# Issuing the K and V loads on ScalarE's queue, with the stores left on SyncE's, in an attention backward kernel

## Chip, cores, metric

One core of a Trainium2 chip. The metric is the device time of one execution in microseconds (us), as the median of several executions. A run counts as slow when it is over 1.5% above the fastest of the same kernel. The experiments ran in several batches; before was run again in each, and its median was 646.2 to 646.4 us every time, so times of different batches can be compared. A ratio is the mean time of one kernel's fast runs over that of the other's in the same rounds, so it is not quite the ratio of the medians that stand beside it.

## The reference

One query row per head attends to 8,192 keys; the kernel returns the output and the gradients of q, k and v.

```python
# B=1, H=32 heads, Sq=1, Skv=8192, Dh=128, all bfloat16
def _fwd_reference(q, k, v):
    scale = q.shape[-1] ** -0.5
    attn = softmax(einsum('bhqd,bhkd->bhqk', q, k) * scale, axis=-1)
    return einsum('bhqk,bhkd->bhqd', attn, v)

def reference(q, k, v, grad_out):
    out, vjp = jax.vjp(_fwd_reference, q, k, v)
    return (out, *vjp(grad_out))          # out, dq, dk, dv
```

K and V (2 MB per head each) are read once, dk and dv (2 MB each) are written once: 268 MB in all, with little arithmetic.

## The kernel before

```python
def load_k(h):                                   # 2 MB; the first head's K in 4 parts
    Kt[h] = kpool.tile([P, NT, D], BF16, ...)    # 3 buffers
    nc.sync.dma_start(slots(Kt[h], c, parts), rows_of(k, h, c, parts))
def load_v(h):
    Vt[h] = vpool.tile([P, NT, D], BF16, ...)    # 2 buffers
    nc.sync.dma_start(Vt[h][:], rows_of(v, h, 0, 1))

# narrow matmuls: 64 + 64 + 64 + 64 of a head's 302
def k_scores(h):     # 64 x (128x128 weights, 4 columns)
    for g in range(CH):
        for c in range(2 * NB):
            nc.tensor.matmul(out[:, g, :], lhsT=cols[:, g, c // 2, c % 2], rhs=q_blk[:, h, c, :], ...)
def v_scores(h, c):  # 4 calls x 16 x (128x128 weights, 2 columns)
    ...
def contract(Xt, rep, out_col, first=0, last=NT):   # for V and for K: 64 x (128x128 weights, 1 column)
    for n in range(first, last):
        nc.tensor.matmul(out_col, lhsT=Xt[:, n, :], rhs=rep[:, n, 0:1], ...)

def outer(h, which, r):            # a quarter of dk or dv on VectorE; the last quarter issues the store
    nc.vector.tensor_tensor(slots(G, r, 4)..., op=ALU.mult)      # G: 2 buffers for dk, 2 for dv
    if r % (4 // parts) == 4 // parts - 1:
        nc.sync.dma_start(rows_of(dst, h, c, parts), slots(G, c, parts))

for h in range(H + 1):             # a software pipeline: head h beside the end of head h-1
    ...                            # K blocks and scores of h; ds, dk and dq of h-1
    if 0 < h and h + 2 < H: load_k(h + 2)
    ...                            # softmax; dk's last quarters and its store
    contract(Vt[h], x["p"], x["m"][:, 2:3])
    ...                            # V transposes and v_scores
    outer(h, "dv", 0); outer(h, "dv", 1); outer(h, "dv", 2)
    if 0 < h and h + 2 < H: load_v(h + 2)
    outer(h, "dv", 3)              # issues dv's store
```

So the one queue carries load V, store dv, load K, store dk, and so on, in turn.

Of the kernel before, what the change touches and what calls it, by code (L numbers as in the profile page):

```python
# [23 lines left out]
def kernel(  # L24
# [11 lines left out]
    nc = tc.nc  # L36
# [23 lines left out]
    Kt, Vt, XK, XV, st = {}, {}, {}, {}, {}  # L60

    def rows_of(x, h, c, parts):
        L = NT // parts
        return x[0, h].rearrange("(p n) d -> p n d", p=P)[:, c * L:(c + 1) * L, :]

    def slots(X, c, parts):
        L = NT // parts
        return X[:, c * L:(c + 1) * L, :]

    def load_k(h):  # L70
        Kt[h] = kpool.tile([P, NT, D], BF16, tag="K", name="Kt")
        parts = NCH if h == 0 else 1
        for c in range(parts):
            nc.sync.dma_start(slots(Kt[h], c, parts), rows_of(k, h, c, parts))

    def load_v(h):
        Vt[h] = vpool.tile([P, NT, D], BF16, tag="V", name="Vt")
        nc.sync.dma_start(Vt[h][:], rows_of(v, h, 0, 1))

    rows = consts.tile([H, 2, D], BF16)  # L80
    nc.sync.dma_start(rows[:, 0, :], q.rearrange("b h s d -> (b h s) d"))
    nc.scalar.dma_start(rows[:, 1, :], grad_out.rearrange("b h s d -> (b h s) d"))
    load_k(0)
    load_v(0)
    load_k(1)
    load_v(1)

    ident = consts.tile([P, P], BF16)
# [166 lines left out]
    for h in range(H + 1):  # L255
# [19 lines left out]
        if 0 < h and h + 2 < H:  # L275
            load_k(h + 2)
# [44 lines left out]
        if 0 < h and h + 2 < H:  # L321
            load_v(h + 2)
# [38 lines left out]
```

## Time and profile before

| | before |
|---|---|
| time, median of 3 (range) | 646.56 us (646.2 to 646.75) |
| profiled span | 644.5 us |
| busiest engine | VectorE, 78% |
| DMA share, 120 to 320 us | 1.01, 428 GB/s |

The prediction below shows the lines that carry this. Two more lines are of use. The first is the chain of work that ended last, by line, in the profile of before: it follows back from the end what each step waited for. The second is from the view of waits (time in total, times, longest).

```profile
DMA Kt<-in_k_dram 48%; DVE XK_sb L146 8%; PE T_ps L183 8%; DMA out_dram<-G_dv 5%; DMA out_dram<-G_dk 5%; PE s_ps L157 5%; DVE G_dk L210 4%; PE dp_ps L200 3%; PE m_ps L200 2%; PE dp_ps L195 2%; ACT XT_sb L185 1%; PE m_ps L294 1%; DVE G_dv L210 1%; PE s_ps L173 1%; DVE sm L163 1%
...
DVE G_dv L210 <- DMA out_dram<-G_dv: 84.6, 25, 4.6
```

The chain runs through a K load and back into the computation that freed its buffer; VectorE also waits for the store of dv two heads ago to free its buffer (84.6 us in 25 waits).

### The profile page before, as it was taken

What the parts mean: (1) busy time and instruction counts of PE and PEld (TensorE: products, weight loads), DVE (VectorE), ACT (ScalarE), POOL (GpSimd) and SP (SyncE); (2) the same over time, 40 slices, a digit from 0 to 9 for tenths busy, and PEclk for the clock granted to TensorE, in tenths of its full rate; (3) what the DMA queues carried; (4) which work ended last, traced back from release to release, by engine and by line L of the source; (5) the groups of instructions that cost most, each with busy time, mean ns of one, the idle gap of its engine ahead of it and who ended that gap; (6) DMA issues with size and microseconds to landing.
All of it is one profiled execution on the core that took longest, in us unless ns stands there. A gap on an engine that the chain in (4) does not pass through costs nothing.

```text
span 644.5 us, 20935 instructions
## 1 busy us (share of the span) xinstructions
PE 481.0 (75%) x9673; PEld 452.0 (70%) x9673; DVE 505.5 (78%) x653; ACT 183.5 (28%) x332; POOL 0.7 (0%) x6
## 2 busy tenths in 40 slices
PE   3898888886677877768777787667786777877780
PEld 2888888886677866768666777667785676866670
DVE  5989899867977779777788777797767977778860
ACT  2333333332233222233222332223322223222230
POOL 0000000000000000000000000000000000000000
PEclk9766666655666655666556666556655666655665
DMA  8999999999999999999999999999999999999985
GB/s 349 407 425 430 424 425 423 429 426 431 427 428 427 427 427 429 429 429 425 433 422 433 425 430 427 427 429 425 427 429 425 431 425 429 429 427 430 424 365 238
DMA packets 19718, 269.80 MB, mean 419 GB/s; under 512 B 2352, under 2 KB 2352, under 8 KB 2864
## 3 DMA queue, kind: packets, MB, share of 16 engines
q1 hardware_dynamic: 19584, 268.47, 98.2%
q8 instruction: 75, 1.23, 0.7%
q14 instruction: 11, 0.09, 0.0%
q10 hardware_dynamic: 48, 0.01, 0.0%
HBM read 134.23 MB, written 134.23 MB: 417 GB/s over the span
## 4 chain that ended last, share of the span: by engine, by line
DMA 59%; PE 21%; DVE 14%; ACT 2%; issue 1%; SPq 0%; DVEq 0%; ACTq 0%
DMA Kt<-in_k_dram 48%; DVE XK_sb L146 8%; PE T_ps L183 8%; DMA out_dram<-G_dv 5%; DMA out_dram<-G_dk 5%; PE s_ps L157 5%; DVE G_dk L210 4%; PE dp_ps L200 3%; PE m_ps L200 2%; PE dp_ps L195 2%; ACT XT_sb L185 1%; PE m_ps L294 1%; DVE G_dv L210 1%; PE s_ps L173 1%; DVE sm L163 1%
## 5 line engine op out<-in xcount | busy, mean ns | idle before, releaser
L210 DVE TENSOR_TENSOR G_dv<-p_rep,qd 128x2048 bf16<-128x2048 bf16 x128 | 148.2, 1221 | 90.3 <-DMA out_dram<-G_dv 84.6
L183 PE MATMUL T_ps<-ident_f,Vt 128*128 128x128 f32 x1024 | 203.4, 382 | 0.2 <-PE m_ps L294 0.2
L183 PEld LDWEIGHTS T_ps<-ident_f,Vt 128*128 128x128 f32 x1024 | 190.7, 210 | 0.2 <-issue 0.2
L185 ACT COPY XT_sb<-T_ps 128x1024 f32<-128x1024 f32 x128 | 128.6, 1013 | 129.3 <-PE T_ps L183 127.2
L210 DVE TENSOR_TENSOR G_dk<-ds_rep,qd 128x2048 bf16<-128x2048 bf16 x128 | 155.6, 1218 | 2.9 <-DMA out_dram<-G_dk 1.9
L146 DVE STREAM_TRANSPOSE XK_sb<-Kt 128x1024 f32<-128x1024 f32 x128 | 148.3, 1214 | 5.8 <-DMA Kt<-in_k_dram 4.7
L157 PEld LDWEIGHTS <-XK_sb 128*128 128x128 bf16 x2048 | 57.7, 104 | 90.7 <-DVE pdt L234 79.9
L157 PE MATMUL s_ps<-q_blk,XK_sb 128*128 128x4 bf16 x2048 | 59.7, 168 | 82.1 <-DVE pdt L234 72.1
L195 PE MATMUL dp_ps<-do_blk,XT_sb 128*128 128x2 bf16 x2048 | 66.7, 164 | 18.1 <-ACT XT_sb L185 18.1
L195 PEld LDWEIGHTS <-XT_sb 128*128 128x128 bf16 x2048 | 64.9, 102 | 20.7 <-ACT XT_sb L185 20.7
L200 PE MATMUL dp_ps<-ds_rep,Kt 128*128 128x1 bf16 x2048 | 64.1, 165 | 1.3 <-issue 1.0
L200 PEld LDWEIGHTS <-Kt 128*128 128x128 bf16 x2048 | 59.6, 104 | 6.8 <-issue 6.6
L244 ACT COPY dq_all<-dp_ps 128x1 f32<-128x1 f32 x32 | 5.1, 159 | 192.4 <-PE dp_ps L200 178.5
L200 PEld LDWEIGHTS <-Vt 128*128 128x128 bf16 x2048 | 57.7, 97 | 0.9
L200 PE MATMUL m_ps<-p_rep,Vt 128*128 128x1 bf16 x2048 | 56.9, 164 | 0.0
L294 PEld LDWEIGHTS m_ps<-rs,ones_f 128*128 128x128 f32 x64 | 16.0, 311 | 49.9 <-ACT e L293 49.9
L294 PE MATMUL m_ps<-rs,ones_f 128*128 128x1 f32 x64 | 18.8, 362 | 40.5 <-ACT e L293 40.5
L303 ACT ACTIVATE p_rep<-e,rinv 128x256 bf16<-128x256 f32 x32 | 16.3, 508 | 30.1 <-DVE rinv L301 30.1
L163 DVE TENSOR_TENSOR sm<-s_ps,in_quad 128x256 f32<-128x256 f32 x32 | 13.6, 424 | 11.1 <-PE s_ps L157 7.9
L229 ACT CAST qd<-s_ps 128x256 bf16<-128x256 f32 x32 | 11.9, 372 | 32.2 <-PE s_ps L225 32.2
L236 DVE SCALAR_TENSOR_TENSOR ds_rep<-dp_ps,pdt,p_s 128x256 bf16<-128x256 f32 x32 | 15.5, 484 | 5.2 <-PE dp_ps L195 2.4
L293 ACT ACTIVATE e<-s_ps,nbias 128x64 f32<-128x64 f32 x32 | 10.0, 313 | 31.8 <-DVE nbias L290 31.8
(44 smaller groups left out, 143.4 us busy)
## 6 DMA issues: line engine op xcount, KB each, us to landing
Vt<-in_v_dram SPq DMA_DIRECT2D x32, 2048.0 KB, 30.0
Kt<-in_k_dram SPq DMA_DIRECT2D x31, 2048.0 KB, 30.8
out_dram<-G_dv SPq DMA_DIRECT2D x30, 2048.0 KB, 34.6
out_dram<-G_dk SPq DMA_DIRECT2D x30, 2048.0 KB, 33.6
out_dram<-G_dv SPq DMA_DIRECT2D x4, 1024.0 KB, 15.0
out_dram<-G_dk SPq DMA_DIRECT2D x4, 1024.0 KB, 13.3
Kt<-in_k_dram SPq DMA_DIRECT2D x4, 512.0 KB, 5.1
out_dram<-fin_sb SPq DMA_DIRECT2D x2, 8.0 KB, 13.1
```

The costliest lines, as they stand in the source:

```text
L146: nc.vector.transpose(XK[h][:, :, :, u, :], slots(Kt[h], u, NCH).rearrange("p g d -> p (g d)").bitcast(F32).rearrange("p (g w j) -> p g w ...
L157: nc.tensor.matmul(out[:, g, :], lhsT=cols[:, g, c // 2, c % 2], rhs=q_blk[:, h, c, :], start=(c == 0), stop=(c == 2 * NB - 1), skip_group ...
L163: nc.vector.tensor_tensor(x["sm"][:], x["s"][:, 0:NT].rearrange("p (a g) -> p a g", a=NQ).unsqueeze(2) .to_broadcast([P, NQ, NCH, CH]), in ...
L183: nc.tensor.transpose(T_ps[:, i, :], words[:, m * P:(m + 1) * P], ident_f[:])
L185: nc.scalar.copy(X[:], T_ps[:])
L195: nc.tensor.matmul(st[h]["dp"][:, n:n + 2], lhsT=X[:, i, e2, :], rhs=do_blk[:, h, e2, :], start=(e2 == 0), stop=(e2 == 1), skip_group_chec ...
L200: nc.tensor.matmul(out_col, lhsT=Xt[:, n, :], rhs=rep[:, n, 0:1], start=(n == 0), stop=(n == NT - 1), skip_group_check=True)
L210: nc.vector.tensor_tensor(slots(G, r, 4).rearrange("p n (a b) -> p n a b", b=R), slots(rep, r, 4).unsqueeze(2).to_broadcast([P, Q, D // R, ...
L229: nc.scalar.copy(x["qd"][:].rearrange("p a d -> p (a d)"), x["s"][:, 256:512])
L236: nc.vector.scalar_tensor_tensor(out=x["ds"][:], in0=x["dp"][:, 0:NT].unsqueeze(2).to_broadcast([P, NT, R]), scalar=pdt[:], in1=x["p_s"][: ...
L294: nc.tensor.matmul(x["m"][:, 0:1], lhsT=ones_f[:], rhs=rs[:], start=True, stop=True, skip_group_check=True)
L303: nc.scalar.activation(x["p"][:], e[:].unsqueeze(2).to_broadcast([P, NT, R]), ACT.Copy, scale=rinv[:])
```

## The change

The intent is that each of the 16 DMA engines finds work in two queues, loads in ScalarE's and stores in SyncE's, and takes from them in turn, rather than a load and a store behind one another in one queue. The first three heads stay as they were.

```diff
     def load_k(h):
...
-            nc.sync.dma_start(slots(Kt[h], c, parts), rows_of(k, h, c, parts))
+            queue = nc.sync if h < 3 else nc.scalar
+            queue.dma_start(slots(Kt[h], c, parts), rows_of(k, h, c, parts))
...
     def load_v(h):
-        nc.sync.dma_start(Vt[h][:], rows_of(v, h, 0, 1))
+        queue = nc.sync if h < 3 else nc.scalar
+        queue.dma_start(Vt[h][:], rows_of(v, h, 0, 1))
```

## The prediction

> **What bounds the kernel now.** I read the page's second part first (busy tenths in 40 slices), because it shows whether one resource is full all the way:
>
> ```profile
> DVE  5989899867977779777788777797767977778860
> DMA  8999999999999999999999999999999999999985
> GB/s 349 407 425 430 424 425 423 429 426 431 427 428 427 427 427 429 429 429 425 433 422 433 425 430 427 427 429 425 427 429 425 431 425 429 429 427 430 424 365 238
> ```
>
> The DMA row is full in 37 of 40 slices; no engine's row is. The rate is flat, 422 to 433 GB/s, except in the first two and last two slices. The queue part then says who carries the bytes:
>
> ```profile
> q1 hardware_dynamic: 19584, 268.47, 98.2%
> q8 instruction: 75, 1.23, 0.7%
> q10 hardware_dynamic: 48, 0.01, 0.0%
> HBM read 134.23 MB, written 134.23 MB: 417 GB/s over the span
> ```
>
> One queue, q1 (all that SyncE issues), is 98.2% of 16 engines' time; half of its bytes are loads, half stores. q10 is ScalarE's, today one 8 KB load. Third, the windows, for the exact DMA share in mid-run and at the end (last two columns: DMA share, GB/s):
>
> ```profile
> 120.00:320.00 200.00, 153.41 (x3040) 144.42 (x3039) 157.41 (x202) 58.23 (x103) 0.00 (x0) 0.59 1.01 428
> 618.00:630.00 12.00, 8.48 (x212) 7.96 (x210) 9.82 (x10) 4.20 (x9) 0.00 (x0) 0.64 0.88 368
> 630.00:640.00 10.00, 0.00 (x0) 0.00 (x0) 0.00 (x0) 0.00 (x0) 0.00 (x0) 0.50 0.72 300
> ```
>
> Share 1.01: the engines have no idle time in mid-run. In the trace's packet records a 16 KB packet takes 611 ns and the next starts about 4 ns before it ends. Fourth, the DMA issues (last column: median us to landing):
>
> ```profile
> Vt<-in_v_dram SPq DMA_DIRECT2D x32, 2048.0 KB, 30.0
> Kt<-in_k_dram SPq DMA_DIRECT2D x31, 2048.0 KB, 30.8
> out_dram<-G_dv SPq DMA_DIRECT2D x30, 2048.0 KB, 34.6
> out_dram<-G_dk SPq DMA_DIRECT2D x30, 2048.0 KB, 33.6
> ```
>
> 2,097,152 bytes at 428 GB/s need 4.9 us, yet landing takes 30 to 35. The four medians sum to 129.0 us per head; the chain's K transposes run from 146.34 to 563.53 over 21 heads, so a head takes 19.87 us, and 129.0/19.87 = 6.5 transfers are in flight on average. The queue never runs dry. Even DVE's largest wait, for a dv store to free its buffer (84.6 us in 25 waits), waits for this backlog.
>
> The bookkeeping: 268.47 MB at 428 GB/s is 627.3 us. Each slice is 16.1 us, so the shortfall against 428 is 3.0 and 0.8 us in the first two slices and 2.4 and 7.1 us in the last two: 13.3. Together 640.6 of 644.5; the rest is slices a little under 428. Without DMA the compute is faster: up to 112 us, where prefetched loads and empty store buffers hide the queue, the chain's K score matmuls repeat every 17.1 us (78.55, 95.65, 112.74).
>
> [...] The trace shows that SyncE's issue time (0.33 us typically) is no limit, with 6.5 transfers in flight. [...]
>
> **The change, part by part.**
>
> *Bytes and packets*: the same. The change moves K and V loads of heads 3 to 31, 2 x 29 = 58 transfers (121.6 MB), from q1 to q10. q1 keeps the first three heads' loads and all stores, about 147 MB.
>
> *SyncE*: 58 issues less, 58 x 0.34 = 20 us. Today it spends its time waiting for buffers, so this is worth 0. A dv store is today issued behind a V load (305.13 after 304.70) and sometimes takes over 1 us for it; it goes out perhaps 0.5 us sooner. With 30 us of queue ahead: 0.
>
> *ScalarE*: 58 issues more. I take SyncE's 0.34 us (ScalarE's own single issue took 0.42): 20 to 24 us over a row of 183.5 us (28% of the span). The place matters[...]. The V load comes after the fourth copy of a V transpose, the K load after the copy of dq:
>
> ```profile
> 304.76 1.01 ACT L185 COPY XT_sb<-T_ps 128x1024 f32<-128x1024 f32 x1 [2.51 <-PE T_ps L183]
> 306.77 0.37 ACT L229 CAST qd<-s_ps 128x256 bf16<-128x256 f32 x1 [1.00 <-PE s_ps L225]
> 313.75 0.16 ACT L244 COPY dq_all<-dp_ps 128x1 f32<-128x1 f32 x1 [6.60 <-PE dp_ps L200]
> 314.90 0.31 ACT L293 ACTIVATE e<-s_ps,nbias 128x64 f32<-128x64 f32 x1 [0.99 <-DVE nbias L290]
> ```
>
> After each there is an idle gap of 1.00 and 0.99 us, and a 0.34 to 0.42 us issue fits in both. What the loads wait for (PE's last reads of the old V and K) is finished by then, as the copy before them waits for later PE work. So ScalarE is not held. The loads leave later: V at 305.8 rather than 304.70, K at 313.9 rather than 313.74: 1.1 and 0.2 us of a 30 us queue, worth 0 while other transfers wait.
>
> *DMA engines*: the only term that can count. Now an engine does 8 load packets, then 8 store packets (one transfer is 128 packets over 16 engines); after, one of each in turn. The switch of direction every 8 packets costs nothing visible today, so I expect none at every packet. [...]
>
> *Start and end*: the first three heads are as before. At the end loads no longer wait behind stores, so the last head may start sooner; but the last stores must still drain, and about nine DMA engines stay busy to the end of the 0.72 window. I give 0 to 2 us.
>
> Sum: 0 - 1 + 0 = about 1 us less: 645.5 us.
>
> **The rivals.**
>
> 1. *Two queues hide per-packet overhead.* [...] Against it: packets already overlap their neighbours by 4 ns, so little is there to hide.
>
> 2. *Alternating costs time.* Each engine has 1,024 packets of 16 KB (268.47 MB/16/16,384), so 13 ns more for each is 13 us: 2% slower, 659. For it: nothing here shows two busy queues, and turning from read to write at each packet could cost what turning at every eighth doesn't show. Against: today's turn is invisible in the share of 1.01. I hold this the likeliest way to miss.
>
> 3. *The order starves compute.* [...] If loads came too late, DVE would wait for K and not for dv. Against: a starved computation issues no stores[...] and compute (17.1 us a head) is faster than DMA (19.87). Worth 0, or 3 to 6 us if transients leave gaps.
>
> 4. *ScalarE becomes a bound.* If an issue took 1.5 us there, 0.5 us would be pushed onto exp, twice a head at most: 1 us x 29 = 29 us of chain, but 19.87 - 17.1 = 2.8 us a head of slack swallows it. Worth 0.
>
> **Range and chances.** [...] I take 638 to 653 as the range. Faster by over 2% (below 633.6)[...]: 0.04. Slower by over 2% (above 659.5): 0.09. Within: 0.87.
>
> **What would show it right or wrong.** In the queue part q10 should carry about 121.6 MB and q1 147, with shares near 45% and 53% if a packet's time stays 611 ns; if each record is stretched by sharing, the shares exceed 100% together while GB/s stays. GB/s in mid-run should be 426 to 430: 433 or more is rival 1, under 420 rival 2. The four landing medians should still sum to about 129 us (same buffers, same head time), but they may split unevenly[...]. The DMA row must stay full; zeros or sevens in mid-run mean rival 3. ScalarE's exp should still wait for nbias and not follow an issue directly. The prediction is wrong if packets slow down when two queues alternate[...].

The sum: 646.5 us of before, 0 for the DMA engines, 1 less for start and end (the middle of 0 to 2), 0 for SyncE and ScalarE, so 645.5 us. Cut, where marked, are general statements on queues and issuing that no trace of before shows, that ScalarE works in order, that the total work stays unchanged whatever the queues hold, an upper rate for the DMA with the times that rival 1 drew from it, equal shares for two queues in rival 3, and a guess at landing times.

## The result, and the profile after

After: 656.52 us median of 4 runs (656.33 to 658.69), beside 646.38 us of before (646.2 to 646.75, 4 runs) in the same rounds. The ratio is 1.0164, with a 95% interval of 1.0142 to 1.0186. The change costs 10 us. It is within 2%, as was thought likeliest, but outside the predicted range of 638 to 653 us.

The slices of the profile after (columns as before):

```profile
DMA  8999999999999999999999999999999999999873
GB/s 342 416 427 427 426 427 427 426 427 428 426 428 427 427 424 426 429 428 428 427 428 426 426 429 424 429 422 426 423 412 422 412 422 428 421 415 424 371 306 162
```

Up to two thirds of the way nothing is to be seen. Then some slices fall to 412, and the last three are 371, 306 and 162, where before had 424, 365 and 238. A slice is 16.4 us long, so against 428 GB/s the last three lack 2.2 + 4.7 + 10.2 = 17.1 us; the same sum for before is 9.7. Most of the 10 us thus lies, in this view, in the last 50 us. The windows say the same in numbers (the last two columns are DMA share and GB/s):

```profile
120.00:320.00 200.00, 147.38 (x3017) 138.47 (x3014) 154.73 (x199) 56.13 (x100) 0.00 (x0) 0.60 1.01 427
618.00:630.00 12.00, 7.32 (x160) 6.53 (x158) 11.30 (x17) 1.45 (x5) 0.00 (x0) 0.50 0.65 272
640.00:655.00 15.00, 1.17 (x35) 0.90 (x31) 3.65 (x4) 0.63 (x3) 0.00 (x0) 0.50 0.38 154
```

The queues carry what was expected, and the four landing medians sum to 121.0 us (129.0 before):

```profile
q1 hardware_dynamic: 11232, 146.83, 53.0%
q10 hardware_dynamic: 8400, 121.65, 44.1%
...
out_dram<-G_dv SPq DMA_DIRECT2D x30, 2048.0 KB, 35.6
out_dram<-G_dk SPq DMA_DIRECT2D x30, 2048.0 KB, 34.7
Kt<-in_k_dram ACTq DMA_DIRECT2D x29, 2048.0 KB, 25.7
Vt<-in_v_dram ACTq DMA_DIRECT2D x29, 2048.0 KB, 25.0
```

Loads now land some 10 us sooner than stores (about 4 us before). The chain has turned accordingly: it no longer goes through K loads but through the stores of dv, one after another. By line, and in order of time (start, us, what):

```profile
DMA out_dram<-G_dv 71%; DVE G_dv L212 11%; PE T_ps L185 4%; DVE G_dk L212 2%; DVE XK_sb L148 2%; PE s_ps L159 2%; PE m_ps L202 1%; DMA Kt<-in_k_dram 1%; PE dp_ps L197 1%; ACT XT_sb L187 1%; PE m_ps L296 0%; DVE sm L165 0%; ACT e L295 0%; DVE nbias L292 0%; ACT qd L231 0%
...
329.54 4.64 DVE G_dv L212 x4
334.20 35.68 DMA out_dram<-G_dv
369.98 4.64 DVE G_dv L212 x4
...
612.76 4.63 DVE G_dv L212 x4
```

A dv store of 35.7 us, then the 4.6 us of VectorE that fill the freed buffer, then its store: this cycle spans two heads. From 329.54 to 612.76 it runs seven times, 283.2/14 = 20.23 us a head, where before needs 19.87. 0.36 us over the 29 heads after the switch is 10.4 us, which is the loss. VectorE's own wait for that store is no longer than before (70.2 us in 18 waits, 84.6 in 25 before): the chain is a loop through the DMA, and waits alone don't show its length.

ScalarE is as predicted. Its timeline in one head:

```profile
301.74 0.16 ACT L246 COPY dq_all<-dp_ps 128x1 f32<-128x1 f32 x1 [7.03 <-PE dp_ps L202]
301.74 0.34 ACTq L75 DMA_DIRECT2D Kt<-in_k_dram  x1
302.94 0.31 ACT L295 ACTIVATE e<-s_ps,nbias 128x64 f32<-128x64 f32 x1 [1.05 <-DVE nbias L292]
```

The issue of the load takes 0.34 us and lies inside a gap; exp still waits for VectorE's nbias.

### What the average of 16 DMA engines hides

The trace records 16 landings of each transfer, read here as one for each DMA engine, and what waits for the transfer waits for the last: of the dv store issued at 334.20 us in after, 15 had landed by 366.85 and the last did at 369.88, and VectorE's G_dv, which had waited 4.10 us for it, starts at 369.98. The landings are recorded by their times and without the engines' numbers; that a place in the order is the same engine each time is read from lags that change slowly from one transfer to the next. Here are the lags of the 16 behind the last (us), for a store of dk at about 300 us and one at about 570 us:

```
before 296  -9.0 -8.8 -8.8 -8.6 -8.6 -7.8 -6.6 -3.2 -2.5 -2.1 -1.9 -1.9 -1.7 -1.7 -0.7  0.0
before 575 -15.5 -15.5 -15.4 -15.3 -15.0 -14.0 -10.6 -3.3 -2.8 -2.8 -2.8 -2.7 -2.7 -2.1 -1.1  0.0
after  304 -16.0 -15.8 -15.7 -14.8 -14.6 -13.8 -13.5 -9.0 -8.3 -8.2 -8.1 -6.4 -6.3 -5.9 -3.5  0.0
after  568 -24.4 -24.3 -24.1 -24.1 -24.1 -23.0 -22.9 -13.2 -12.8 -12.3 -11.9 -10.4 -10.3 -10.0 -7.6  0.0
```

There are three groups in after: seven fast engines, eight that are 10 to 17 us later, and **one alone** that ends 7.6 us behind the next. Before, two groups and no engine alone. The landing times of the last engine advance by 9.95 us per pair of transfers before (a load and a store, 8 packets of each on that engine) and by 10.15 us after. The second to last engine takes 9.94 before and 9.91 after. So one engine of 16 became slower by 2%, and every transfer waits for it. The others keep the average full until they run out of work at the end; that is why share and GB/s in mid-run look untouched (1.01 and 427).

For the eight middle engines e8 shows a cause. The queue part lists q8, the fetching of TensorE's instructions, with 75 packets of 16 KB (14 in e6, where most narrow matmuls are cut, and none in e1, where TensorE has no work). That is 1.23 MB for the 19,346 instructions of TensorE, about 64 bytes each, and a packet takes 1.0 us in the packet records, before and after. In e8 below, 47 such packets put eight engines 8.7 us behind, 1.5 us for each packet that one of the eight takes. At that rate 75 packets cost each of the eight an estimated 14 us; the row of before at 575 has them about 12.5 us behind the seven.

### The profile page after: what moved, and what is told of

Its sections match the earlier page's. It is cut to its first block, busy times and chain, and to the rows that moved or that the text cites. A ratio compares the mean times of both kernels' runs of the same rounds, so it can differ in the third digit from the quotient of the medians.

```text
span 654.6 us, 20883 instructions
## 1 busy us (share of the span) xinstructions
PE 479.8 (73%) x9673; PEld 450.2 (69%) x9673; DVE 501.8 (77%) x653; ACT 183.8 (28%) x332; POOL 0.7 (0%) x6
## 3 DMA queue, kind: packets, MB, share of 16 engines
q10 hardware_dynamic: 8400, 121.65, 44.1%
q8 instruction: 75, 1.23, 0.7%
## 4 chain that ended last, share of the span: by engine, by line
DMA 72%; DVE 16%; PE 9%; ACT 1%; issue 1%; DVEq 0%; SPq 0%; ACTq 0%
DMA out_dram<-G_dv 71%; DVE G_dv L212 11%; PE T_ps L185 4%; DVE G_dk L212 2%; DVE XK_sb L148 2%; PE s_ps L159 2%; PE m_ps L202 1%; DMA Kt<-in_k_dram 1%; PE dp_ps L197 1%; ACT XT_sb L187 1%; PE m_ps L296 0%; DVE sm L165 0%; ACT e L295 0%; DVE nbias L292 0%; ACT qd L231 0%
## 5 line engine op out<-in xcount | busy, mean ns | idle before, releaser
L212 DVE TENSOR_TENSOR G_dv<-p_rep,qd 128x2048 bf16<-128x2048 bf16 x128 | 148.2, 1220 | 107.9 <-DMA out_dram<-G_dv 70.2
L202 PEld LDWEIGHTS <-Kt 128*128 128x128 bf16 x2048 | 59.6, 104 | 6.0 <-issue 5.9
L238 DVE SCALAR_TENSOR_TENSOR ds_rep<-dp_ps,pdt,p_s 128x256 bf16<-128x256 f32 x32 | 15.5, 484 | 5.3 <-PE dp_ps L197 2.5
```

Of the source, the lines that this page charges most:

```text
L212: nc.vector.tensor_tensor(slots(G, r, 4).rearrange("p n (a b) -> p n a b", b=R), slots(rep, r, 4).unsqueeze(2).to_broadcast([P, Q, D // R, ...
L238: nc.vector.scalar_tensor_tensor(out=x["ds"][:], in0=x["dp"][:, 0:NT].unsqueeze(2).to_broadcast([P, NT, R]), scalar=pdt[:], in1=x["p_s"][: ...
```

## The experiments

The first theory was **S**: alternating loads and stores packet by packet costs time by itself. Its rivals were F, that the fetching of instructions makes the one engine late, and C. After e1 to e4 came **P**: something that TensorE does in its bursts of narrow matmuls stretches the packets of one DMA engine, above all its stores, and the new order exposes more stores to it. P came from the packet records of after: packets of the late engine that took 50 to 100 ns over the normal 611 lay in the bursts of narrow matmuls, while in the phase of the V transposes they kept to 607 ns from start to start. The letter C stands for the rival that the loss comes with the two queues and the kernel's order, whatever TensorE does. Labels are those of the runs.

### Transfers alone, in one queue and in two (e1, e2)

```diff
 for h in range(H):           # the same 128 transfers of 2 MB, no computation: outputs wrong on purpose
-    nc.sync.dma_start(Kt[:], rows_of(k, h))      # e1_dma_one
+    nc.scalar.dma_start(Kt[:], rows_of(k, h))    # e2_dma_two
     nc.sync.dma_start(rows_of(out_3, h), G[:, 1])
-    nc.sync.dma_start(Vt[:], rows_of(v, h))
+    nc.scalar.dma_start(Vt[:], rows_of(v, h))
     nc.sync.dma_start(rows_of(out_2, h), G[:, 0])
```

> Only the transfers, no computation (wrong results on purpose): every head's K and V loaded, and two constant tiles stored, all on SyncE's queue, a load and a store in turn. Theory S (one slow DMA engine: with load packets and store packets alternating one by one, one of the 16 loses about 24 ns at each packet, the others nothing): nothing alternates one by one here, so the last engine takes about 4.86 to 4.95 us a transfer, 128 transfers, 625 to 637 us in all. Rival F (instruction fetches fall on one engine and make it late): there are hardly any fetches here, so near 625 us. Rival C (the computation's order costs the time, not the DMA engines): the same, about 625 to 630.

> The same transfers without computation, loads on ScalarE's queue and stores on SyncE's. Theory S: one engine needs 10.1 us for 8 load and 8 store packets and the others 9.72, so 64 such pairs take 646 to 650 us, at least 10 us more than e1, and the last landing of a late transfer comes over 10 us after the other 15. Rivals F and C: no difference from e1 (within 2 us), landings of all 16 within 3 us, because there are neither fetches nor computation.

Measured: e1 637.01 us (ratio to before 0.9854, 0.984 to 0.9869), e2 630.88 us (0.976, 0.9746 to 0.9775). Two queues are not slower; e1's 6 us more lie at its start, where the loads stand in the one queue behind a first store that is issued only at 9.4 us, once VectorE has filled its tile. After that both take 9.72 to 9.74 us per pair of transfers on every engine, and the 16 landings lie within 3.5 us (e1) and 2.4 us (e2). The GB/s row of e2:

```profile
GB/s 332 430 429 431 429 430 433 433 430 431 430 430 431 430 433 432 431 431 429 432 430 430 433 432 431 430 430 432 430 430 433 432 432 429 430 432 431 429 433 353
```

S falls: alternating by itself costs nothing. The prediction's reason was right for packets alone. And 9.72 against 9.95 says that even before loses something to its computation.

### Only V's loads, and the change from the middle on (e3, e4)

```diff
 # e3_v_only: load_k stays on SyncE; load_v as in the change
-            queue = nc.sync if h < 3 else nc.scalar      # e4_half, both loads
+            queue = nc.sync if h < 17 else nc.scalar
```

> The changed kernel with the K loads back on SyncE: only V loads on ScalarE's queue. Theory S: V packets alternate with SyncE's packets for 16 of the 32 packets of a head on an engine, half as many as in the changed kernel, so about half its loss: 650 to 653 us. Rival F: the loss does not depend on how many transfers alternate: 656. Rival C (loads overtake stores and the stores come too late at the end): V loads still overtake, K loads not; 648 to 656, not told apart.

> The changed kernel with the switch to ScalarE's queue at the eighteenth head (15 heads of loads there instead of 29). Theory S: the loss goes with the number of heads: 15/29 of 10 us, so 651 to 652 us. Rival C (a cost of the end, or of loads that overtake stores once): the end is as in the changed kernel, so 655 to 657.

Measured: e3 652.93 us (1.0104, 1.0087 to 1.0121), e4 655.71 us (1.0145, 1.013 to 1.016), both correct. Half of the loads moved cost 6.5 of the 10 us. The switch at the half cost nearly all of them, where a cost per packet would have made it some 651 to 652 us; this is what C expected, and e6 decides on C. In e4 the last engine's pair takes 9.93 us up to the switch and 10.17 after, and at 569 us it is alone, 9.8 us behind the next. The loss thus doesn't add up packet by packet. Our reading is that what an engine lost counts only from the time at which it is the last: in after the one engine is 0.2 to 0.6 us behind the next for the stores issued at 173 to 212 us, and 7.2 at 557. No run tests this by itself.

### The kernels with few narrow matmuls (e5, e6)

```diff
-        for g in range(CH):
-            for c in range(2 * NB):
-                nc.tensor.matmul(out[:, g, :], ...)                   # 64
+        nc.tensor.matmul(x["s"][:, 0:NT], lhsT=cols[:, CH - 1, 0, 0], rhs=q_blk[:, 0:CH, 0, :], ...)   # 1
-        for i in range(CH // 2):  ... for e2 in range(2):             # v_scores: 64 a head
+        nc.tensor.matmul(st[h]["dp"][:, c * CH:(c + 1) * CH], ...)    # 4 a head
-        for n in range(first, last):                                  # contract: 128 a head
+        for n in (first, last - 1):                                   # 6 a head
```

The same edit on before (e5) and on after (e6); all else stays; outputs wrong. The last line is 2 for V and 2 for each half of K.

> The kernel before with three of TensorE's loops of narrow matmuls cut from 64, 64 and 128 a head to 1, 4 and 4 (wrong results on purpose); all transfers and the rest stay. Theory P (one DMA engine is slowed in its store packets while TensorE runs its dense loops of narrow matmuls; a load packet alone is not slowed): that engine is no longer late, so the last landing of a late store comes within 12 us of the first instead of 15; 638 to 644 us. Rival C (order of the computation): no change of the DMA side, 643 to 647.

> The changed kernel with the same three loops cut. Theory P: the slow engine is gone, so two queues cost no more than one: within 3 us of e5, 636 to 645 us, and no single engine over 4 us behind the other 15. Rival C (loads overtake stores and the end comes late): the loss stays, 8 to 10 us above e5.

Measured: e5_before_few 636.85 us (0.9854, 0.9838 to 0.9871), e6_after_few 637.27 us (0.9861, 0.9847 to 0.9876). The whole 10 us of the change are gone: the two orders are within 0.4 us. Both are also 9.5 us faster than before (e5 came out 1.2 us below P's range). No engine is alone in e6 (the last is 2.1 us behind the next at 574 us, the first 7.4 ahead), and q8 has 14 packets rather than 75. The end of e6's GB/s row has no trough before its last slice:

```profile
GB/s 337 425 423 433 430 432 433 428 430 427 430 435 428 434 428 428 429 432 432 430 429 430 431 429 432 430 429 433 430 428 431 433 428 434 430 429 429 428 409 257
```

This is as P says, and not C: without the narrow matmuls two queues cost nothing in the kernel either. It doesn't yet say why before is spared, and since the fetching went too, it is left to e8 to show that the one late engine isn't late by fetching. The chain of e6 still runs through the stores of dv (75% of the span), so the chain's turn in after is not by itself the loss. Nor are the 9.5 us P's alone: 61 fetch packets fewer, at e8's 1.5 us on one of eight engines, are an estimated 11 us on each of the eight, and in before those end within 3.3 us of the last. How the 9.5 us divide between fetching and stretched stores isn't separated.

### Matmuls put beside the bare transfers (e7, e9)

```diff
 for h in range(H):           # e7_dma_two_pe: e2 with these; e9_dma_one_pe: e1 with these
+    for n in range(300):
+        nc.tensor.matmul(acc[:, n % 8:n % 8 + 1], lhsT=W[:, n % 8, :], rhs=W[:, 0, 0:1], start=True, stop=True)
```

They read and write nothing that the transfers touch, and nothing waits for them; outputs wrong.

> e2 (transfers alone, loads and stores on two queues, 630.9 us) with 9,600 narrow matmuls on constant tiles, that depend on no transfer and take the first 270 us or so. Theory P: one engine falls behind by some 60 ns a packet while they run, 15 to 28 us in all, and the end moves by as much: 644 to 660 us. Rivals C and F: no dependence on transfers, so 631 to 634 (the fetches of 19,200 instructions alone are 75 packets of 1 us over 16 engines).

> Transfers only, all on SyncE's one queue, loads and stores in turn, with the same 9,600 independent narrow matmuls as e7; outputs wrong on purpose. Theory P (a stream of narrow matmuls stretches the store packets of one DMA engine, on whatever queue): the matmuls run nearly all the time here and are not in step with the stores, so the one engine should fall behind at the rate of e7, some 20 to 25 us by the time they end: 652 to 662 us. Rival (only two queues in turn expose it): 637 to 643 us, like e1_dma_one.

Measured: e7 654.45 us (1.0126, 1.0111 to 1.0142), 23.6 us over e2; e9 657.1 us (1.0167, 1.0152 to 1.0183), 20.1 us over e1. TensorE's row and the GB/s row of e7:

```profile
PE   3454646464655555555556465564640000000000
...
GB/s 332 426 427 426 427 424 429 428 427 424 425 427 426 428 428 427 424 427 425 427 428 429 421 427 427 424 429 428 428 422 429 434 434 432 432 425 432 433 317 73
```

The rate rises when the matmuls stop, after slice 30. The lags of stores of e7 and e9 behind their last engine (issued at, lag of the first, of the second to last):

```
e7   147 -9.0 -2.0 | 270 -15.4 -5.3 | 393 -21.7 -8.6 | 454 -24.5 -8.5 | 573 -24.6 -8.8
e9   141 -8.4 -0.1 | 264 -14.5 -3.5 | 388 -21.6 -6.2 | 449 -24.1 -7.2 | 567 -24.1 -7.3
```

One engine falls behind steadily while the matmuls run, to some 24 us, and hardly at all afterwards (24.5 us, then 24.6 in e7). It does so in one queue as in two. So independent narrow matmuls make one DMA engine late, and two queues are not a condition. They must expose the kernel to it in some other way.

### Loads apart from stores (e8)

```diff
+# e8_phases: all 64 loads, then all 64 stores, in SyncE's queue; 6,000 of e7's matmuls beside each half
```

> Transfers alone, first all 64 loads, then all 64 stores, on one queue; TensorE runs 6,000 narrow matmuls at the start of the loads and 6,000 at the start of the stores. Theory P, from the stalls read in the trace of the kernel before: in the loads no engine falls behind by more than 3 us; in the stores one engine falls behind by 70 to 80 ns for each packet in the first 170 us, 15 to 22 us in all, then no further: 640 to 652 us. If loads were slowed as well, an engine would be late by over 8 us at the end of the loads.

Measured: 659.69 us (1.0209, 1.0193 to 1.0224), outputs wrong. This is 7.7 us above P's range, and engines were late by over 8 us at the end of the loads, which was to show that loads are slowed as well. The lags at the end of the loads and late in the stores:

```
loads  297  -9.5 -9.3 -9.2 -9.2 -9.2 -9.0 -8.9 -8.8 -1.4 -0.5 -0.2 -0.2 -0.2 -0.1 -0.1  0.0
stores 581 -29.0 -28.8 -28.6 -28.4 -28.4 -28.2 -28.0 -13.3 -13.3 -13.2 -12.6 -12.3 -12.0 -12.0 -11.8  0.0
```

During the loads eight engines together fall behind by 9 us, in steps of 1.5 us that follow the fetch packets, and none is alone. During the stores one engine, until then among the fast ones, goes to the very end and 11.8 us behind the next. The single engine is late because of its **stores**. The rate agrees: against the seven fastest it lost 28 us over 12,000 instructions, 2.3 ns each, where e7's lost 24.6 over 19,200, 1.3 ns each, and in e7 only half of its packets are stores. Only this run separates them: where two queues alternate, the time of a stretched packet stands now with the loads' queue (e16: 461 us over 611 ns per packet, against 43 in the stores' queue), now with the stores' (e12: 378 against 61), so a packet's record there doesn't say which of the two was held up.

### The order of before, with a head's two stores in a row (e11)

If only stores suffer, it matters which packets the late engine has in hand during a burst. In the trace of before, the late engine's load packets in bursts (110.4 to 115.3 and 130.6 to 135.5 us) are stretched by 0 to 8 ns, and its store packets in a burst (124.6 to 129.3) by 14 to 160 ns. The bursts follow the computation, which at times waits for the landing of a store (VectorE's G_dv for dv's: 84.6 us in 25 waits), thus for that very engine, whose next packets in the queue's order are a load. So before may be spared by its phase, that is, by which packets the bursts happen to meet. This run moves the phase and keeps the one queue:

```diff
             c = r // (4 // parts)
+            if parts == 1 and which == "dv":
+                return
+            if parts == 1:                       # dk: dv's store first, then dk's own
+                nc.sync.dma_start(rows_of(out_3, h, 0, 1), slots(x["dv"], 0, 1))
             nc.sync.dma_start(rows_of(dst, h, c, parts), slots(G, c, parts))
```

> The kernel before, all on SyncE's queue, with each head's two stores issued one right after the other (order load, load, store, store); correct result. Theory P with phase (before, the bursts of narrow matmuls happen to fall on load packets): the first burst of a head now falls on store packets, and some 0.3 to 0.6 us per head is lost: 652 to 662 us. Rival (two queues are needed for the loss): 644 to 649 us.

Measured: 657.17 us (1.0165, 1.0149 to 1.018), correct: the loss of the change, to the microsecond, without a second queue. The queue part and the GB/s row:

```profile
GB/s 348 408 429 426 426 430 427 426 426 426 429 427 428 426 428 427 428 428 429 426 429 424 421 413 416 422 420 422 401 428 418 406 426 401 425 423 413 424 342 151
...
q1 hardware_dynamic: 19584, 268.47, 97.5%
```

The row has late troughs like after's, from somewhat earlier on, and much the same end. The dk store issued at 567.5 us has one engine alone, 7.1 us behind the next, and a head takes 20.3 us (264.0 us over 13 heads). The last landings of 120 to 600 us show where the time went. In e11 they advance by 4.85 and 4.89 us for a load, as in before (4.87 and 4.90), but by 5.10 us for a store of dv and 5.47 for one of dk (5.05 and 5.06 before). That dv's store is issued later is not the reason: every store of that stretch was issued at least 26 us before it landed, so the last engine had work all the time. The second queue was one way among others to lose the phase of before.

### Which work it is: many instructions or a busy engine (e10, e12, e13, e16)

```diff
 # each is e2 with this work per head in place of e7's 300 matmuls (not 320, as the first expectation has it)
+nc.tensor.matmul(acc[:], lhsT=W[:, n % 8, :], rhs=W[:, 0:4, :], ...)        # e10_dma_two_wide: 32 of 512 columns
+nc.vector.tensor_copy(small[:, n % 8:n % 8 + 1], W[:, n % 8, 0:1])          # e12_dma_two_dve: 290 of 128x1
+nc.vector.tensor_copy(small[:], W[:])                                       # e13_dma_two_dve_wide: 29 of 128x1024
+nc.vector.tensor_copy(small[:, m:m + 1], W[:, n % 8, 0:1])                  # e16_dve_no_semaphores: as e12, each its own column
```

> e2_dma_two with 32 matmuls of 512 columns per head in place of e7's 320 narrow ones, so that TensorE is busy with a tenth of the instructions; outputs wrong on purpose. If the number of TensorE's instructions is what stretches the packets: 630 to 634 us and no lone straggler. If it is TensorE being busy: 645 us or more.

> e2_dma_two with 290 tiny VectorE copies per head in place of the matmuls of e7; outputs wrong on purpose. If the cause is TensorE's instructions: 630 to 634 us, no lone straggler. If any engine's dense instruction stream does it: 640 us or more.

> e12_dma_two_dve with 29 VectorE copies of 128x1024 per head in place of 290 of 128x1: a tenth of the instructions, VectorE still busy most of the time; outputs wrong on purpose. If the number of instructions stretches the packets: 630 to 634 us and no lone straggler. If VectorE's work itself does it: 645 us or more.

> e12_dma_two_dve with every one of the 9,280 copies writing its own column, so that no copy waits for or updates a semaphore; outputs wrong on purpose. If the instruction itself costs what it costs on TensorE (1.2 ns): 638 to 648 us. If a VectorE copy costs 6 ns whatever it does with semaphores: 680 to 692 us. If only semaphore updates cost: 630 to 634 us.

The groups of e10, e12 and e13, in that order (busy time, mean ns of one):

```profile
L64 PE MATMUL acc<-W 128*128 128x512 bf16 x1024 | 223.1, 381 | 10.0 <-DVE W L56 10.0
```

```profile
L64 DVE COPY small<-W 128x1 bf16<-128x1 bf16 x9280 | 563.6, 146 | 0.0
```

```profile
L64 DVE COPY small<-W 128x1024 bf16<-128x1024 bf16 x928 | 396.2, 427 | 32.0
```

| run | work beside e2's transfers | time, us | ratio (95%) | over e2, us | per instruction |
|---|---|---|---|---|---|
| e7 | 9,600 narrow matmuls, 19,200 instructions | 654.45 | 1.0126 (1.0111, 1.0142) | 23.6 | 1.2 ns |
| e10 | 1,024 wide matmuls, 2,048 instructions | 632.87 | 0.9791 (0.9775, 0.9807) | 2.0 | no late engine |
| e12 | 9,280 small copies | 692.93 | 1.0727 (1.068, 1.0774) | 62.1 | 6.7 ns |
| e13 | 928 large copies | 635.65 | 0.9836 (0.9822, 0.9849) | 4.8 | 5.1 ns |
| e16 | 9,280 small copies without semaphores | 690.52 (3 fast runs) | 1.066 (1.0632, 1.0688) | 59.6 | 6.4 ns |

TensorE is busy for nearly as long in e10 as in e7 (223 and 267 us of matmuls), yet in e10 the 16 landings stay within 3.3 us and no engine is alone; its 2.0 us over e2 are not of this kind. In e13 one engine is alone, 4.0 us behind the next when the copies end. The loss goes with the number of instructions, not with the busy time. I had expected TensorE alone to do it: e12 refutes that. VectorE's copies cost one engine even more, and in e13 a tenth of them costs about a tenth, so they go by the number too (e13 came out 1.7 us above the range of the first expectation, and with the lone straggler that it had excluded). In the stores issued from 416 us on, the last engine of e12 lags 35 us behind the other 15. In e12 every copy also waited for a semaphore and updated it (11,709 updates in the trace, 2,431 in e16); e16 shows no cost of this beyond the spread of the two (690 to 697 and 687 to 694 us).

What about an instruction does it stays open. Fetching is not enough: e12's 73 fetch packets took about 0.31 us each, 23 us if all fell on that one engine, against 62 lost. Another suspect couldn't be taken away, the recording of the instructions for the profile; no run here shows that it costs anything. Every timed run here left a span and a clock as well, so we take every one to have been recorded, and no run tells executing an instruction from recording it.

### A correct kernel with fewer TensorE instructions (e14, e15)

```diff
-        for n in range(first, last):
-            nc.tensor.matmul(out_col, lhsT=Xt[:, n, :], rhs=rep[:, n, 0:1], ...)          # 64 x 1 column
+        for n in range(first, last, 2):
+            nc.tensor.matmul(wide, lhsT=rep[:, n:n + 2, 0], rhs=Xt[:, n:n + 2, :] ..., ...)  # 32 x 256 columns
+ # then a copy of [2, 256] to SBUF and two small matmuls that add its two halves into out_col
```

> The kernel before with the two contractions of a head done by 32 matmuls of 256 columns each in place of 64 of one column (two small matmuls then add the two halves): about 120 of a head's 604 TensorE instructions go; correct result. If the time lost to the instruction stream (9.5 us by e5) goes down with the instructions: 642 to 645 us. If not, or if the wider matmuls cost as much as they save: 646 to 650 us.

> The same on the changed kernel; correct result. The change's loss (10 us, with 9 more under it by e6) should fall in proportion to the bursts that are thinned, two of a head's four: 646 to 652 us, and the lone straggler drifts about half as fast. If the loss doesn't depend on the density of instructions: 655 to 658 us.

Measured: e14 676.97 us (1.0479, 1.0464 to 1.0493), e15 675.83 us (1.0462, 1.0442 to 1.0481), both correct, both a clear miss. The chain of e14 by engine says why:

```profile
PE 80%; ACT 15%; issue 2%; DMA 1%; DVE 1%; SPq 0%; ACTq 0%; DVEq 0%
```

TensorE became the bound: a contraction's 32 matmuls of 256 columns take 334 ns each for K where the 64 of one column took 165, and TensorE is busy for 88% of the span, in spite of a higher granted clock (0.92, against 0.60 before). The question of the run was not answered. It does show one thing more: where the DMA isn't the bound, the two orders differ by 1.1 us, within the noise (the intervals of their ratios overlap), and from 400 us on the 16 landings stay within 5.9 us. No version that beats both kernels was found; of the two kernels, before is the better.

## Why the prediction was wrong, point by point

- **What bounds the kernel**: right that it is the DMA, but read from the mean of 16 engines. Before's landing records have 9.95 us per pair and two groups of engines up to 15.5 us apart; bare transfers (9.72) and e5 (9.5 us less) then showed what that costs. The prediction put it down to slices "a little under 428".
- **Bytes and packets, SyncE, ScalarE**: right. q10 carries 121.65 MB, issues take 0.34 us in gaps of about 1 us, exp waits for nbias.
- **DMA engines**, the step that failed: "The switch of direction every 8 packets costs nothing visible today, so I expect none at every packet". The first half holds for transfers alone (e2: 9.72 us per pair, ratio 0.976). "So" doesn't hold in the kernel: the order of packets decides whether stores or loads of one engine meet TensorE's bursts (e11 shows the loss with one queue, e6 and e7 that the bursts do it; that before's order owes its speed to its phase rests on its packet records and on e11's outcome). The term was 0 and measured 10 us, 0.36 us a head. That the total work stays unchanged was a second reason for it. It would not have been enough: in after the mean does stay full (share 1.01, 427 GB/s in mid-run), but the last of 16 landings comes 24.4 us behind the first (at 568 us).
- **Start and end**, given as 0 to -2 us: wrong in sign in this view, since the end is where 15 engines wait for the one. It is the same loss, not a second one.
- **Rival 1** (hidden overhead): transfers alone took 6 us less in two queues (e2, 630.88 us) than in one, but these lie at e1's start; after it both take 9.72 to 9.74 us per pair. The kernel with two queues took 656.52 us.
- **Rival 2** (alternating costs) was called the likeliest way to miss and named the right sign and nearly the size (13 us against 10), with a mechanism that e2 refutes; that its number comes near is chance. Its own test, GB/s under 420 in mid-run, didn't fire: 427.
- **Rivals 3 and 4**: out. The DMA row stays full (share 1.01 in mid-run), and ScalarE isn't held (exp still waits 1.05 us for nbias).
- **The landing medians**: expected to sum to about 129 and to split unevenly; they sum to 121.0, with loads at about 25 and stores at about 35 us.
- **The range**: 638 to 653 was put around a term of zero for the DMA engines, with too little beyond for how they are fed.

## What to carry to other kernels

When the DMA is the bound, look at the 16 landings of a transfer and not only at DMA share and GB/s: one late engine sets the pace while the average stays full (after: 7.6 us behind the next at 568 us, share 1.01, 10 us lost). A queue's order can be tuned without anyone having meant it; moving transfers between queues, or only two stores together, can lose that (ratios 1.0164 for the change, 1.0165 for e11), so measure the change even where bytes, packets and issue times say nothing. Long streams of tiny instructions aren't free for a kernel bound by its transfers, even when nothing waits for them (e7: 23.6 us over e2): part is the fetching of the instructions, part lands on the stores of one engine (e5: 9.5 us for both). We take all runs here to have been recorded, so whether the second part exists in a run without recording isn't known.
